# Turning the second product of the first layer: tokens stationary for five of six blocks, and another issue plan

## The chip, the cores and the metric

The kernel runs on one core of a Trainium2 chip. The time is device microseconds of one execution; the kernel before has a median of 624.69 us over three runs (620.73 to 627.0). A profiled execution of it took 617.57 us, of which 615.9 us lie between its first and its last instruction (the span).

## The reference, cut to what matters

Three layers follow one another. A delta-rule attention runs over 768 steps for 2 x 8 heads of width 48 and yields x, 1536 tokens by 384. The first layer is a dense one with a rational activation:

```
h = x @ w_in                        # 1536 x 384 by 384 x 2048
P = a[0] + a[1]*h + a[2]*h*h + a[3]*h*h*h
Q = 1 + |b[0]|*|h| + |b[1]|*h*h
g = P / (Q + 1e-6)
x = g @ w_out                       # the second product: 1536 x 2048 by 2048 x 384
```

The second layer sends each token to one of 8 experts by the argmax of x @ w_gate, and computes gate * (relu(x @ w1[e]) @ w2[e]) for it. Every token's row has to be known before the last expert lists are complete.

## The kernel before, in words

**Attention.** The sequence is cut into 12 chunks of 64 steps. Groups of four chunks share a triangular solve on VectorE (solve, L249, 31 pairs of operations per group, lines L264 and L267). Then every chunk runs a chain of small TensorE products (lower, tk, qk, u, s, y, x), with ScalarE copies between them. x_mm (L387) puts the result of a chunk, split in a high and a low f16 part, into the block's x tiles, with features on the partitions.

**First layer.** Two chunks make a block of 256 tokens; there are six blocks. A block has eight tiles, each of two groups of 128 hidden features (w_in's columns) by 256 tokens. Per tile, s1 runs 18 f16 matmuls of 256 columns (L454); ScalarE, GpSimd and VectorE evaluate the rational function (steps s1, e2, e3), and e3 splits g into gh (ScalarE, L481) and gl = g - gh (GpSimd, L482), both f32r, with hidden features on the partitions and tokens along the free axis. s2 (L485) runs the second product: for each of three groups of 128 output features and each of the two hidden groups, three matmuls (wo_h with gh, wo_h with gl, wo_l with gh), 18 of 256 columns each. The stationary operand is a 128x128 piece of w_out, the moving one is g. Two of the three accumulators share a PSUM bank, which a matmul of zeros over 512 columns (L493) opens. After the eighth tile three ScalarE copies (L505) bring the block's result to x2, features on partitions.

**Weights of the first layer.** w_in and w_out come as float64 and are taken apart by conv (L194) in 16 pieces: four VectorE operations (L189, L190, L191, L199), two ScalarE copies (L198, L201) and one GpSimd subtraction (L202) each. conv_load (L181) brings a piece into a ring of two tiles by a DMA of SyncE's queue, so a later load waits for an earlier piece's conversion. Tile number t of block 0 needs pieces 2t and 2t+1.

**Gate.** gate (L507) is a generator of five steps per block. It multiplies x2 by w_gate (L516, features are the contraction, so x2's layout fits), finds the expert of each token, counts places (place, L567), turns x2 into rows of tokens with six transposes (L547) into PSUM, scales each row by a power of two and writes the rows to DRAM (SyncE DMA). After the last block's gate the expert lists are read back and gathered by row.

**Experts.** 16 DMAs, ScalarE casts (L702) and VectorE subtractions (L703) bring the weights of the first two experts ahead of time, during blocks 4 and 5; their early lists are settled after gate 3 (settle, L615). The others are loaded behind the last list. Each expert has hp products (L746, 256 columns) and y products (L783, 384 columns).

**Order.** All steps up to the last block stand in a dictionary with a time from PLAN, sorted by that time at L949; a step first issues what it needs. The times are only numbers to sort by. The program is then built under a tile framework that arranges the instructions of each engine by a simulated timeline, with the issue order as priority, so that instructions of several steps are mixed on one engine; on the chip every engine works in the order so fixed. In PLAN, `tiles` holds for each block the time of its first tile and the step between tiles, `lags` those of e2, e3 and s2 behind s1, `u` the times of the chunks, `rel` those of a chunk's other steps around it, `solve` the start and the step of each of the three solves, `conv` start and step of pieces 2 to 15, `early` pieces 0 and 1, `lead` how far a load stands ahead of its conversion, `w` the early expert weights, `pre` and `settle` the early experts. behind (L837) also ties a conversion's instructions to the end of an earlier solve: piece 2 to that of solve 0, pieces 3 to 15 to that of solve 1.

Of the kernel before, what the change touches and what calls it, by code (L numbers as in the profile page):

```python
# [7 lines left out]
F32 = mybir.dt.float32  # L8
# [4 lines left out]
AF = mybir.ActivationFunctionType  # L13
# [10 lines left out]
DM = H * D  # L24
# [6 lines left out]
ROW = DM + 1  # L31
BLOCKS = [range(i, i + 2) for i in range(0, 12, 2)]
XS = 0.125
PLAN = {'tiles': ((87.83, 6.95), (160.76, 6.97), (189.73, 5.73), (233.4, 5.29), (280.51, 3.83), (328.46, 2.58)),
 'lags': (8.77, 6.68, 15.19),
 'u': (51.36, 70.55, 88.09, 99.81, 109.31, 135.51, 158.51, 197.55, 219.65, 238.81, 250.88, 281.51),
 'rel': {'kT': 2.63,
         'loads': 4.47,
         'values': -10.66,
         'qk': -3.8,  # L40
         'lower': -5.93,
         'tk': -2.67,
         's': 2.76,
         'y': 2.44,
         'x': 5.8},
 'norm': (-34.08, 36.43, 112.73),
 'solve': ((-7.06, 3.69), (20.76, 8.26), (160.31, 5.92)),
 'gram': ((-1.03, 1.43), (15.51, 2.1), (124.49, 9.18)),
 'qk': (10.43, 33.11),
 'conv': (58.99, 3.27),  # L50
 'early': (8.24, 14.14),
 'lead': 16.47,
 'gate': (1.01, 2.5),
 'w': (354.93, 2.35),
 'experts': 2,
 'behind': 3,
 'masks': 2,
 'copies': 1,
 'settle': 298.54,
 'pre': ((342.38, 356.18, 337.4, 357.65), (326.4, 369.59, 380.06, 389.43)),  # L60
 'hold': 1}
WN = 4
CA = 2
# [12 lines left out]
def attention_moe_moe(ctx, tc, kT, qT, k, v, beta, w_io, a, b, w_gate, w1, w2, out, dbg=None):  # L76
    nc = tc.nc
# [4 lines left out]
    st = ctx.enter_context(tc.tile_pool(name="st", bufs=2))  # L82
# [3 lines left out]
    ps_a = ctx.enter_context(tc.tile_pool(name="ps_a", bufs=2, space=PSUM))  # L86
# [4 lines left out]
    def slot(shape, dt, name):  # L91
        return slots.tile(shape, dt, tag="slot", name=name)
# [7 lines left out]
    wo_h = slot([128, 16, DM], F32R, "wo_h")  # L100
    wo_l = slot([128, 16, DM], F32R, "wo_l")
# [31 lines left out]
    def load_kk(r):  # L133
        kk = st.tile([128, 2, 16, D], F32, tag="raw", name="kk", bufs=2)
        for i in range(2):
            kks[r, i] = kk[:, i]
            nc.sync.dma_start(kks[r, i], k[:, 4 * r + 2 * i:4 * r + 2 * i + 2].rearrange("p c u d -> p (c u) d"))
# [10 lines left out]
    ident = const.tile([128, 128], F32, name="ident")  # L148
# [124 lines left out]
    ends = {}  # L273

    def lower(n, tile_):
# [6 lines left out]
        for p in range(2):  # L282
            lo, hi = slice(64 * p, 64 * p + 32), slice(64 * p + 32, 64 * p + 64)
            for sl, o in ((lo, 0), (hi, 32)):
                if n < PLAN["copies"]:
                    nc.gpsimd.tensor_copy(Z[sl, :, p, o:o + 32], Wu[sl, :, us].rearrange("p t u -> p u t"))
# [46 lines left out]
    def qk(n, tile_):  # L333
# [6 lines left out]
        for p in range(2):  # L340
            o = slice(64 * p, 64 * p + 64)
            if n < PLAN["masks"]:
                nc.vector.tensor_tensor(G[o, :, p, :], g[o], mask[o].unsqueeze(1).to_broadcast([64, NP, C]), ALU.mult)
# [65 lines left out]
    wg = const.tile([128, 3, E], F32, name="wg")  # L409
# [24 lines left out]
    acc, ghl, x2t = {}, {}, {}  # L434
# [50 lines left out]
    def s2(i):  # L485
        blk, js_ = TILES[i]
        w = 512 // len(js_)
        gh, gl = ghl.pop(i)
        if js_[0] == 0:
            pair = ps_a.tile([128, 2, 256], F32, tag="acc", name="acc")  # L490
            acc[blk] = [pair[:, 0], pair[:, 1], ps_a.tile([128, 256], F32, tag="acc", name="acc2")]

            nc.tensor.matmul(pair.rearrange("p a (c b) -> p a c b", c=2), low16[0:1, 0:1].to_broadcast([1, 128]), ones16[0:1].unsqueeze(1).to_broadcast([1, 4, 128]).rearrange("p (a c) b -> p a c b", a=2), start=True, stop=False)  # L493
        for dt in range(3):
            ds_ = slice(128 * dt, 128 * dt + 128)
            for k_, j in enumerate(js_):
                for m, (ww, g) in enumerate(((wo_h, gh), (wo_h, gl), (wo_l, gh))):
                    ends["s2"] = nc.tensor.matmul(  # L498
                        acc[blk][dt][:, 0:w], ww[:, j, ds_], g[:, w * k_:w * k_ + w], start=(dt == 2 and j == 0 and m == 0), stop=(dt > 0 and j == 15 and m == 2)
                    )  # L500
        if js_[-1] == 15:
            x2 = st.tile([128, 3, 256], F32, tag="t64", name="x2", bufs=3)
            x2t[blk] = [x2[:, dt] for dt in range(3)]
            for dt in range(3):
                nc.scalar.activation(x2t[blk][dt], acc[blk][dt], AF.Copy)  # L505

    def gate(blk, tile_, tile_x, tile_p):  # L507

        nt = len(BLOCKS[blk])
        pr = BLOCKS[blk][0] // 2  # L510
        hp = nt // 2
        x2 = x2t.pop(blk)
        lp = tile_([128, nt, E], "lp")
        for i in range(nt):
            for dt in range(3):
                nc.tensor.matmul(lp[:, i, :], x2[dt][:, 128 * i:128 * i + 128], wg[:, dt, :], start=(dt == 0), stop=(dt == 2))  # L516
        lg = sm.tile([128, nt, E], F32, tag="lg", name="lg")
        m = sm.tile([128, nt, 6], F32, tag="m", name="m")

        def bc(i):  # L520
            return m[:, :, i:i + 1].to_broadcast([128, nt, E])

        eib = ei.unsqueeze(1).to_broadcast([128, nt, E])
        w = sm.tile([128, nt, E], F32, tag="w", name="w")
        nc.vector.tensor_reduce(m[:, :, 0:1], lp, AX, ALU.max)
        nc.vector.tensor_tensor(w, lp, bc(0), ALU.is_equal)
        nc.vector.tensor_tensor(w, w, eib, ALU.mult)
        nc.vector.tensor_reduce(m[:, :, 1:2], w, AX, ALU.min)
        oh4 = oh.rearrange("p (b i) e -> p b i e", b=2)[:, :, pr:pr + hp]
        nc.vector.tensor_tensor(  # L530
            oh4, bc(1).rearrange("p (b i) e -> p b i e", b=2), eib.rearrange("p (b i) e -> p b i e", b=2), ALU.is_equal
        )
        nc.vector.tensor_tensor(lg, lp, bc(0), ALU.subtract)
        pl = place(blk, tile_p)
        next(pl)
        nc.scalar.activation(lg, lg, AF.Exp)
        nc.vector.tensor_reduce(m[:, :, 2:3], lg, AX, ALU.add)
        nc.vector.tensor_scalar(m[:, :, 2:3], m[:, :, 2:3], 1e-9, None, ALU.add)
        nc.vector.reciprocal(m[:, :, 2:3], m[:, :, 2:3])
        yield  # L540
        if blk < len(BLOCKS) - 1:
            next(pl)
            yield
        for i in range(nt):
            xp = tile_x([128, DM], "xp2")
            for dt in range(3):
                nc.tensor.transpose(xp[:, 128 * dt:128 * dt + 128], x2[dt][:, 128 * i:128 * i + 128], ident)  # L547
            tt = 6 * (i // hp) + pr + i % hp
            mx = m[:, i, 3:4]
            nc.vector.tensor_reduce(mx, xp, AX, ALU.max, apply_absolute_value=True)  # L550
            nc.vector.tensor_scalar(mx, mx, 2.0 ** -100, None, ALU.max)
            nc.vector.tensor_scalar(mx.bitcast(U32), mx.bitcast(U32), 0x7F800000, None, ALU.bitwise_and)
            nc.vector.reciprocal(m[:, i, 4:5], mx)
            xr = sm.tile([128, ROW], F32, tag="xr", name="xr")
            nc.scalar.activation(xr[:, 0:DM], xp, AF.Copy, scale=m[:, i, 4:5])
            nc.vector.tensor_scalar(xr[:, DM:ROW], m[:, i, 2:3], 1.0 / (MS * MS), mx, ALU.mult, ALU.mult)
            nc.sync.dma_start(rows[128 * tt:128 * tt + 128, :], xr)
            if dbg is not None:
                nc.sync.dma_start(dbg["x2"][128 * tt:128 * tt + 128, :], xr[:, 0:DM])
                nc.sync.dma_start(dbg["sc"][:, tt:tt + 1], mx, allow_slow_non_contiguous=True)  # L560
            yield
        if blk == len(BLOCKS) - 1:
            next(pl)
        yield
# [248 lines left out]
    def add(name, time, needs, f):  # L813
        todo[name] = (time, needs, f)
# [10 lines left out]
    first = {blk: next(i for i in range(len(TILES)) if TILES[i][0] == blk) for blk in range(len(BLOCKS))}  # L825
    tiles_at, lags = PLAN["tiles"], PLAN["lags"]
    T = [tiles_at[blk][0] + (i - first[blk]) * tiles_at[blk][1] for i, (blk, _) in enumerate(TILES)]
    U = PLAN["u"]
    r0 = PLAN["rel"]
    early = NCH and U[1] + r0["x"]  # L830
# [17 lines left out]
    add(("kk", 1), 2.0, [], lambda: load_kk(1))  # L848
    add(("kk", 2), PLAN["norm"][2] - 8, [("norm", 1)], lambda: load_kk(2))
    gens = {r: solve(r) for r in range(3)}  # L850
# [41 lines left out]
    for blk in range(len(BLOCKS)):  # L892
        last = blk == len(BLOCKS) - 1
        i = first[blk] + sum(t[0] == blk for t in TILES) - 1
# [86 lines left out]
    with tc.If(over > SLOTS):  # L981
# [3 lines left out]
        for e in range(E):  # L985
            run(weights(e, got2))
            for t0, nt in ((0, 2), (2, 1)):
                x = expert_x(gather(e, t0, nt, idx3), a_tile)
# [61 lines left out]
```

## Time and profile before

| | us |
|---|---|
| median of three runs | 624.69 (620.73 to 627.0) |
| profiled execution | 617.57 |
| its span | 615.9 |
| TensorE matmul busy (6197 instructions) | 520.5, 85% of the span |
| TensorE weight loads busy | 438.9, 71% |
| VectorE busy (868) | 470.8, 76% |
| ScalarE busy (773) | 396.2, 64% |
| GpSimd busy (282) | 289.2, 47% |
| mean granted TensorE clock | 0.953 of full speed |

The busy time of TensorE is of pipelined matmuls, each recorded from its start to its modelled end; what a matmul costs in a row of them is the distance from start to start. PE is the matmul side of TensorE, PEld its weight loads, DVE VectorE, ACT ScalarE, POOL GpSimd, SP SyncE. The granted clock is 1.00 at 2.4 GHz and 0.50 at 1.2 GHz.

### The profile page before, as it was taken

The page shows a single profiled execution, that of the slowest core. Times are in us where ns is not written, and L with a number is a line of the kernel's source. Part 1 is how long each engine was busy: PE and PEld are TensorE (multiplying, and loading weights), DVE is VectorE, ACT ScalarE, POOL GpSimd, SP SyncE. Part 2 cuts the span into 40 slices and gives each one's busy share as a digit, 9 for nine tenths or more (in the row PEclk, how much of TensorE's full clock was granted, in tenths as well). Part 3 has the DMA queues.
Part 4 walks back from the last instruction along what each step waited for, and adds up shares of the span by engine and source line. Part 5 has one row for each costly group of instructions (what it writes and reads, how often), then busy time and mean ns, then how long its engine had stood idle before and what let it go on. Part 6 is the DMA issues. An engine that isn't in the chain of part 4 may idle for free.

```text
span 615.9 us, 15199 instructions
## 1 busy us (share of the span) xinstructions
PE 520.5 (85%) x6197; PEld 438.9 (71%) x6197; DVE 470.8 (76%) x868; ACT 396.2 (64%) x773; POOL 289.2 (47%) x282
## 2 busy tenths in 40 slices
PE   5514995787998999887999999988897799799993
PEld 5514773576777988776888888878786687577761
DVE  4999999999886799997486367899965588873320
ACT  6844665777799776559868779877662477661110
POOL 8402115966965475455576445747752231212111
PEclk9999997889698899998999999989999699999998
DMA  9901313744621002010000100651002798861000
GB/s 254 262 28 56 88 41 108 199 142 129 190 98 41 1 1 57 12 40 1 14 15 28 28 15 20 201 174 59 27 27 93 223 298 281 280 219 41 16 17 30
DMA packets 42159, 59.33 MB, mean 96 GB/s; under 512 B 25550, under 2 KB 29172, under 8 KB 42082
## 3 DMA queue, kind: packets, MB, share of 16 engines
q1 hardware_dynamic: 40034, 52.78, 28.8%
q0 software_dynamic: 2048, 5.52, 2.7%
q8 instruction: 50, 0.82, 0.5%
q14 instruction: 27, 0.22, 0.1%
HBM read 52.76 MB, written 6.30 MB: 96 GB/s over the span
## 4 chain that ended last, share of the span: by engine, by line
DVE 34%; PE 31%; ACT 12%; DMA 9%; issue 7%; POOL 4%; SPq 0%; POOLq 0%; ACTq 0%; DVEq 0%
PE y L783 7%; DVE A L264 7%; PE acc L498 6%; DVE A L267 6%; PE hp L746 6%; PE h L454 5%; DMA ws<-in_w_dram 5%; DVE h L473 2%; DVE pf L464 2%; ACT A L288 2%; DVE pf L463 2%; DVE ew L703 2%; DVE pf L472 2%; DVE t L190 2%; ACT ew L702 2%
## 5 line engine op out<-in xcount | busy, mean ns | idle before, releaser
L454 PE MATMUL h<-x,wi 128*128 128x256 f16 x864 | 114.2, 280 | 15.8 <-ACT wi L198 7.4
L454 PEld LDWEIGHTS <-wi 128*128 128x128 f16 x864 | 79.8, 100 | 32.3 <-ACT wi L198 8.1
L482 POOL TENSOR_TENSOR gl<-pf,gh 128x512 fp32r<-128x512 f32 x48 | 65.1, 1357 | 63.4 <-ACT gh L481 59.5
L498 PE MATMUL acc<-gl,wo_h 128*128 128x256 f32 x288 | 85.9, 302 | 2.0 <-POOL gl L482 2.0
L498 PE MATMUL acc<-gh,wo_h 128*128 128x256 f32 x288 | 83.7, 306 | 1.7 <-ACT gh L481 1.7
L498 PE MATMUL acc<-gh,wo_l 128*128 128x256 f32 x288 | 83.1, 292 | 0.0
L703 DVE SCALAR_TENSOR_TENSOR ew<-ws,ew 128x768 f16<-128x768 f32 x64 | 62.2, 986 | 12.8 <-ACT ew L702 12.7
L461 POOL TENSOR_SCALAR zf<-za,cf 128x512 f32<-128x512 f32 x48 | 44.3, 924 | 51.1 <-ACT za L459 50.6
L702 ACT ACTIVATE ew<-ws 128x768 f16<-128x768 f32 x64 | 52.5, 841 | 20.7 <-DMA ws<-in_w_dram 20.1
L462 POOL TENSOR_TENSOR zf<-zf,za 128x512 f32<-128x512 f32 x48 | 64.2, 1337 | 3.4
L746 PE MATMUL hp<-dx,ew 128*128 128x256 f16 (+1 forms) x576 | 60.7, 268 | 4.9 <-DVE hl L752 4.4
L746 PEld LDWEIGHTS <-ew 128*128 128x128 f16 x576 | 52.9, 102 | 12.1 <-issue 5.6
L498 PEld LDWEIGHTS acc<-gl,wo_h 128*128 128x128 f32 x288 | 57.7, 200 | 3.7 <-POOL gl L482 2.8
L498 PEld LDWEIGHTS acc<-gh,wo_h 128*128 128x128 f32 x288 | 55.4, 199 | 4.5 <-ACT gh L481 2.6
L498 PEld LDWEIGHTS acc<-gh,wo_l 128*128 128x128 f32 x288 | 57.8, 201 | 0.3
L783 PE MATMUL y<-ew,hh 128*128 128x384 f16 x224 | 56.1, 327 | 0.0
L789 POOL DMA_INDIRECT out_dram<-yo,idx x16 | 18.0, 1124 | 77.0 <-DVE yo L787 62.7
L472 DVE SCALAR_TENSOR_TENSOR pf<-pf,cf,h 128x512 f32<-128x512 f32 x48 | 35.5, 740 | 19.0 <-ACT h L471 18.8
L264 DVE TENSOR_TENSOR A<-A,A 128x31 f32<-128x31 f32 (+15 forms) x93 | 42.9, 461 | 2.5
L463 DVE TENSOR_TENSOR pf<-pf,h 128x512 f32<-128x512 f32 x48 | 32.6, 680 | 13.2 <-ACT pf L460 13.2
L267 DVE TENSOR_TENSOR A<-A,A 128x31 f32<-128x31 f32 (+15 forms) x93 | 40.4, 434 | 2.4
L470 ACT ACTIVATE za<-zf,qc 128x512 f32<-128x512 f32 x48 | 34.5, 719 | 11.4 <-POOL zf L462 11.2
(174 smaller groups left out, 1199.3 us busy)
## 6 DMA issues: line engine op xcount, KB each, us to landing
ws<-in_w_dram SPq DMA_DIRECT2D x64, 384.0 KB, 3.9
raw<-in_w_io_dram SPq DMA_DIRECT2D x16, 768.0 KB, 4.0
rows<-xr SPq DMA_DIRECT2D x12, 192.5 KB, 2.4
kk<-in_k_dram SPq DMA_DIRECT2D x6, 384.0 KB, 4.6
A<-in_k_dram SPq DMA_DIRECT2D x24, 96.0 KB, 3.1
v<-in_v_dram SPq DMA_DIRECT2D x12, 192.0 KB, 3.9
A<-in_qT_dram SPq DMA_DIRECT2D x24, 96.0 KB, 2.7
A<-in_kT_dram SPq DMA_DIRECT2D x10, 192.0 KB, 3.8
```

The lines of the kernel that those rows point to most:

```text
L264: nc.vector.tensor_tensor(tmp, A[:, j, n:32].unsqueeze(2).to_broadcast([128, m, n]), T[:, j:n, 0:n].to_broadcast([128, m, n]), ALU.mult)
L267: nc.vector.tensor_tensor(T[:, n:32, 0:n], T[:, n:32, 0:n], tmp, ALU.add)
L454: s1_last[i] = nc.tensor.matmul(h[:, w * m:w * m + w], ww[:, kt, js], x[:, kt, 0:w], start=(n == 0), stop=(n == 8))
L462: nc.gpsimd.tensor_tensor(zf, zf, za, ALU.mult)
L463: nc.vector.tensor_tensor(pf, pf, h, ALU.mult)
L472: nc.vector.scalar_tensor_tensor(pf, pf, cf[:, 0:1], h, ALU.add, ALU.mult)
L482: nc.gpsimd.tensor_tensor(gl, pf, gh.bitcast(F32), ALU.subtract)
L498: ends["s2"] = nc.tensor.matmul(acc[blk][dt][:, 0:w], ww[:, j, ds_], g[:, w * k_:w * k_ + w], start=(dt == 2 and j == 0 and m == 0), stop= ...
L702: nc.scalar.activation(ws[:, 2 * m, cs], s, AF.Copy, scale=MS)
L703: nc.vector.scalar_tensor_tensor(ws[:, 2 * m + 1, cs], s, MS, ws[:, 2 * m, cs], ALU.mult, ALU.subtract)
L746: nc.tensor.matmul(hp[:, g, 0:ns], w[:, kt, 128 * (f + g):128 * (f + g) + 128], xx[:, kt, 0:ns], start=(n == 0), stop=(n == 8))
L783: nc.tensor.matmul(y, hx[f // 4][:, f % 4, cs], w[:, f, :], start=(n == 0), stop=(n == 23))
```

## The change

For blocks 0 to 4 the second product is turned. The stationary operand is now a piece of gh or gl (128 hidden features by 128 tokens), the moving operand is a whole row block of w_out (128 hidden features by 384 output features). A tile then has 12 matmuls of 384 columns where it had 18 of 256. They run in the order wo_h with gh, wo_l with gh, wo_h with gl. The result has tokens on partitions: two accumulators of 384 columns, each a PSUM tile of its own, no matmul of zeros, and two ScalarE copies to x2 where there were three.

The gate of such a block begins with a new first step: six transposes of x2 and two ScalarE copies of 384 columns into xT, which the product with w_gate then reads. The six transposes that stood later in the gate fall away; the row steps read x2 in SBUF and no longer a PSUM tile. The gate keeps five steps: transposes; gate product and expert; counting; both row groups; the rest. Block 5 is computed and gated as before.

PLAN gets other numbers throughout. Sorted, they put conversions 3 to 13 ahead of the y, s and x steps of chunks 0 and 1 (before, they stood among the chunk steps), the steps of solve 2 3.59 apart instead of 5.92, so that its end stands ahead of s2 of tile 11 and no longer behind that of tile 16, block 0's first tile behind chunk 2's x step, settle behind s2 of tile 37 instead of tile 32, and the early expert weights closer together. A moved conversion takes its DMA load with it.

```diff
--- before.py
+++ after.py
@@ -31,33 +31,35 @@
 ROW = DM + 1
 BLOCKS = [range(i, i + 2) for i in range(0, 12, 2)]
 XS = 0.125
-PLAN = {'tiles': ((87.83, 6.95), (160.76, 6.97), (189.73, 5.73), (233.4, 5.29), (280.51, 3.83), (328.46, 2.58)),
- 'lags': (8.77, 6.68, 15.19),
- 'u': (51.36, 70.55, 88.09, 99.81, 109.31, 135.51, 158.51, 197.55, 219.65, 238.81, 250.88, 281.51),
- 'rel': {'kT': 2.63,
-         'loads': 4.47,
+
+BYTOK = range(5)
+PLAN = {'tiles': ((94.62, 6.95), (151.99, 6.94), (188.36, 5.73), (232.03, 5.29), (276.15, 3.92), (344.39, 2.58)),
+ 'lags': (8.77, 6.68, 15.4),
+ 'u': (50.59, 69.78, 81.54, 98.48, 107.98, 124.54, 157.18, 195.04, 218.05, 237.74, 249.51, 282.48),
+ 'rel': {'kT': 2.41,
+         'loads': 4.55,
          'values': -10.66,
          'qk': -3.8,
          'lower': -5.93,
          'tk': -2.67,
-         's': 2.76,
-         'y': 2.44,
-         'x': 5.8},
- 'norm': (-34.08, 36.43, 112.73),
- 'solve': ((-7.06, 3.69), (20.76, 8.26), (160.31, 5.92)),
- 'gram': ((-1.03, 1.43), (15.51, 2.1), (124.49, 9.18)),
- 'qk': (10.43, 33.11),
- 'conv': (58.99, 3.27),
- 'early': (8.24, 14.14),
+         's': 10.18,
+         'y': 3.45,
+         'x': 7.22},
+ 'norm': (-36.92, 54.42, 110.21),
+ 'solve': ((-5.44, 3.69), (31.55, 6.74), (156.04, 3.59)),
+ 'gram': ((-1.03, 1.72), (14.91, 1.55), (123.21, 9.13)),
+ 'qk': (10.43, 32.45),
+ 'conv': (58.22, 0.02),
+ 'early': (8.43, 7.71),
  'lead': 16.47,
  'gate': (1.01, 2.5),
- 'w': (354.93, 2.35),
+ 'w': (364.51, 1.45),
  'experts': 2,
  'behind': 3,
  'masks': 2,
  'copies': 1,
- 'settle': 298.54,
- 'pre': ((342.38, 356.18, 337.4, 357.65), (326.4, 369.59, 380.06, 389.43)),
+ 'settle': 310.33,
+ 'pre': ((362.66, 372.11, 354.38, 372.47), (338.34, 382.38, 397.83, 407.42)),
  'hold': 1}
 WN = 4
 CA = 2
@@ -486,6 +488,22 @@
         blk, js_ = TILES[i]
         w = 512 // len(js_)
         gh, gl = ghl.pop(i)
+        if blk in BYTOK:
+            if js_[0] == 0:
+                acc[blk] = [ps_a.tile([128, DM], F32, tag="acc", name="acct") for _ in range(2)]
+            for m, (ww, g) in enumerate(((wo_h, gh), (wo_l, gh), (wo_h, gl))):
+                for t in range(2):
+                    for k_, j in enumerate(js_):
+                        o = w * k_ + 128 * t
+                        ends["s2"] = nc.tensor.matmul(
+                            acc[blk][t], g[:, o:o + 128], ww[:, j, :], start=(j == 0 and m == 0), stop=(j == 15 and m == 2)
+                        )
+            if js_[-1] == 15:
+                x2 = st.tile([128, 2, DM], F32, tag="t64", name="x2", bufs=3)
+                x2t[blk] = x2
+                for t in range(2):
+                    nc.scalar.activation(x2[:, t], acc[blk][t], AF.Copy)
+            return
         if js_[0] == 0:
             pair = ps_a.tile([128, 2, 256], F32, tag="acc", name="acc")
             acc[blk] = [pair[:, 0], pair[:, 1], ps_a.tile([128, 256], F32, tag="acc", name="acc2")]
@@ -510,10 +528,26 @@
         pr = BLOCKS[blk][0] // 2
         hp = nt // 2
         x2 = x2t.pop(blk)
+        if blk in BYTOK:
+            xT = st.tile([128, 2, DM], F32, tag="t64", name="xT", bufs=3)
+            for i in range(nt):
+                xp = tile_x([128, DM], "xp2")
+                for dt in range(3):
+                    nc.tensor.transpose(xp[:, 128 * dt:128 * dt + 128], x2[:, i, 128 * dt:128 * dt + 128], ident)
+                nc.scalar.activation(xT[:, i], xp, AF.Copy)
+            yield
+
+            def col(i, dt):
+                return xT[:, i, 128 * dt:128 * dt + 128]
+        else:
+
+            def col(i, dt):
+                return x2[dt][:, 128 * i:128 * i + 128]
+
         lp = tile_([128, nt, E], "lp")
         for i in range(nt):
             for dt in range(3):
-                nc.tensor.matmul(lp[:, i, :], x2[dt][:, 128 * i:128 * i + 128], wg[:, dt, :], start=(dt == 0), stop=(dt == 2))
+                nc.tensor.matmul(lp[:, i, :], col(i, dt), wg[:, dt, :], start=(dt == 0), stop=(dt == 2))
         lg = sm.tile([128, nt, E], F32, tag="lg", name="lg")
         m = sm.tile([128, nt, 6], F32, tag="m", name="m")
 
@@ -542,9 +576,12 @@
             next(pl)
             yield
         for i in range(nt):
-            xp = tile_x([128, DM], "xp2")
-            for dt in range(3):
-                nc.tensor.transpose(xp[:, 128 * dt:128 * dt + 128], x2[dt][:, 128 * i:128 * i + 128], ident)
+            if blk in BYTOK:
+                xp = x2[:, i]
+            else:
+                xp = tile_x([128, DM], "xp2")
+                for dt in range(3):
+                    nc.tensor.transpose(xp[:, 128 * dt:128 * dt + 128], col(i, dt), ident)
             tt = 6 * (i // hp) + pr + i % hp
             mx = m[:, i, 3:4]
             nc.vector.tensor_reduce(mx, xp, AX, ALU.max, apply_absolute_value=True)
@@ -558,7 +595,8 @@
             if dbg is not None:
                 nc.sync.dma_start(dbg["x2"][128 * tt:128 * tt + 128, :], xr[:, 0:DM])
                 nc.sync.dma_start(dbg["sc"][:, tt:tt + 1], mx, allow_slow_non_contiguous=True)
-            yield
+            if blk not in BYTOK or i:
+                yield
         if blk == len(BLOCKS) - 1:
             next(pl)
         yield
```

## Rows read from the trace of the kernel before

**Rows 1.** Busy time by stretch, us; (x) counts; then granted clock, DMA share, GB/s.

```profile
92.00:168.00 76.00, 58.72 (x811) 47.44 (x810) 73.82 (x85) 55.57 (x118) 55.28 (x41) 0.84 0.51 154
168.00:222.00 54.00, 50.97 (x648) 44.71 (x644) 42.75 (x82) 47.97 (x98) 33.45 (x34) 0.94 0.15 42
222.00:282.00 60.00, 53.56 (x704) 46.02 (x702) 59.14 (x107) 37.46 (x77) 31.43 (x30) 1.00 0.11 28
282.00:290.00 8.00, 5.58 (x85) 4.86 (x86) 4.90 (x8) 7.84 (x15) 3.90 (x4) 0.93 0.01 2
290.00:400.00 110.00, 109.52 (x1446) 96.50 (x1446) 72.96 (x146) 88.76 (x176) 65.47 (x67) 0.99 0.15 45
400.00:440.00 40.00, 33.01 (x276) 29.28 (x275) 39.50 (x79) 28.34 (x51) 26.60 (x28) 0.96 0.33 100
440.00:464.00 24.00, 24.00 (x234) 21.87 (x234) 15.81 (x33) 14.78 (x27) 11.50 (x10) 1.00 0.07 25
482.00:541.00 59.00, 53.98 (x483) 44.07 (x483) 49.41 (x76) 40.96 (x64) 15.09 (x13) 0.93 0.85 267
```

**Rows 2.** The chain that ended last, in order of time: start, length, what.

```profile
275.46 1.06 DVE A L264
...
315.87 2.59 PE acc L498 x20
...
473.15 7.79 DMA xd<-rows,idx
...
557.76 7.80 PE y L783 x48
```

**Rows 3.** The second product alone (L498) by stretch: PE busy, PEld busy, counts, clock.

```profile
92.00:168.00 76.00, 15.32 (x90) 13.12 (x90) 0.84 0.51 154
168.00:222.00 54.00, 17.38 (x109) 15.86 (x109) 0.94 0.15 42
282.00:290.00 8.00, 0.70 (x3) 0.70 (x4) 0.93 0.01 2
290.00:400.00 110.00, 43.33 (x295) 37.81 (x295) 0.99 0.15 45
```

**Rows 4.** Timeline of PE: start, us, engine, line, operation, count.

```profile
290.53 0.41 PE L498 MATMUL acc<-gl,wo_h 128*128 128x256 f32 x1
290.75 0.41 PE L498 MATMUL acc<-gh,wo_l 128*128 128x256 f32 x1
...
296.20 0.94 PE L454 MATMUL h<-x,wi 128*128 128x256 f16 x7
297.06 0.32 PE L359 MATMUL U<-A,A 112*64 112x48 f32 x2
...
309.28 1.50 PE L516 MATMUL lp<-wg,x 128*128 128x8 f32 x12
...
311.22 0.28 PE L498 MATMUL acc<-gl,wo_h 128*128 128x256 f32 x1
311.34 0.28 PE L498 MATMUL acc<-gh,wo_l 128*128 128x256 f32 x1
```

**Rows 5.** All engines by stretch, as in Rows 1, around the first timeline rows.

```profile
290.00:292.00 2.00, 2.00 (x11) 2.00 (x11) 2.00 (x4) 1.92 (x5) 1.63 (x3) 0.50 0.00 0
```

**Rows 6.** Groups by line: busy us, mean ns; idle before, releaser.

```profile
L498 PE MATMUL acc<-gl,wo_h 128*128 128x256 f32 x288 | 85.9, 302 | 2.0 <-POOL gl L482 2.0
...
L505 ACT ACTIVATE x<-acc 128x256 f32<-128x256 f32 x18 | 5.9, 381 | 4.4 <-PE acc L498 4.3
L385 ACT ACTIVATE ys<-Y 128x384 f32<-128x384 f32 x12 | 5.8, 480 | 0.4 <-PE Y L383 0.3
```

**Rows 7.** One conversion's four VectorE operations (of the same view).

```profile
L191 DVE SCALAR_TENSOR_TENSOR t<-raw,t 128x768 uint32<-128x768 uint32 x16 | 20.3, 1271 | 0.1
L190 DVE SCALAR_TENSOR_TENSOR t<-raw,t 128x768 uint32<-128x768 uint32 x16 | 18.6, 1169 | 0.1
L199 DVE SCALAR_TENSOR_TENSOR wi<-t,wi 128x384 f16<-128x384 f32 x16 | 15.6, 975 | 0.1
L189 DVE TENSOR_SCALAR t<-raw 128x768 uint32<-128x768 uint32 x16 | 13.4, 845 | 1.3 <-DMA raw<-in_w_io_dram 1.3
```

**Rows 8.** The first product alone (L454) by stretch, as Rows 3.

```profile
92.00:168.00 76.00, 17.63 (x108) 9.53 (x105) 0.84 0.51 154
```

## The prediction

> **What bounds the kernel now.** I begin with the busy times by stretch, because no engine bounds the whole span. From 92 to 168 us DVE works 73.8 of 76 us [rows 1]: there the conversions of the weights stand beside block 0's tiles, and PE has 17 us to spare. From 168 to 222 PE works 51.0 of 54 and DVE only 42.8. From 222 to 282 DVE is full again (59.1 of 60), with solve 2 among the tiles. Then comes the stretch that matters most: from 290 to 400 PE is busy for 109.5 of 110 us, DVE for 73.0 and ACT for 88.8. From 400 to 440 DVE has 39.5 of 40 (expert weights beside tiles), from 440 to 464 PE has all of it, with block 5 alone left [rows 1]. The chain that ended last says the same in order of time: solve operations of DVE up to 275, PE rows such as 20 matmuls of L498 in one piece at 315.9, the gather of the last list at 473.2, expert products at the end [rows 2]. What lies behind the gather (482 to 541 with DMA at 0.85 of its share [rows 1], then products) is not touched; it starts when block 5's gate ends. So the question is how much earlier block 5's gate ends.
>
> **Part 1, the product itself.** Its price is the distance from start to start, not the recorded 0.28 us. At full clock it is 311.34 - 311.22 = 0.120 us for 256 columns [rows 4], so a tile's 18 matmuls take 2.16 us. For 384 columns there is no f32r row. The nearest is the experts' y product, 384 columns of f16 with a weight load for each: 7.80 / 48 = 0.1625 us [rows 2]. That is the lower end: 12 x 0.1625 = 1.95 us. The upper end scales the 0.120 with the columns, 0.180 us, and 12 x 0.180 = 2.16 us, no gain at all. Which end is near depends on what the 0.120 is made of, stream or weight load. Two rows bear on it. At the half clock (granted 0.50 [rows 5]) the distance is 290.75 - 290.53 = 0.22, so the stream of 256 columns sets it there (256 / 1.2 GHz = 0.213); at full clock the stream alone would be half of that, 0.107, and 0.120 is more. And the gate product streams 8 columns only, yet 12 of its f32 matmuls start about (1.50 - 0.28) / 11 = 0.111 us apart [rows 4] (0.28, the length of one recorded matmul, stands for the last one's tail): a load of 128 f32 columns costs about that by itself. So 0.120 is a weight load with little added, and under 384 columns it hides. I take 0.1625: 0.21 us saved per tile, 8.4 us over 40 tiles at full clock. At half clock nothing is saved (18 x 0.213 = 12 x 0.320).
>
> The Trainium skill ("TensorE: Matmul & The Clock Gate", section LDWEIGHTS) gives a load of 128 columns 107 ns, and its section "Back-to-back issue gap" gives 256 columns 109 ns and 384 columns 162.5. By these figures both forms of a tile would take 1.95 to 1.96 us and the part would gain nothing. The trace disagrees for f32r: 0.120, not 0.109 [rows 4]; the measurement decides, and what stands above uses the rows alone.
>
> How much of it is open? Where DVE is full, PE time saved is waiting time. I count the second product in the stretches where DVE is not full: 109 + 3 + 295 matmuls [rows 3], which is 407 / 18 = 22.6 tiles, all of blocks 0 to 4. That is 22.6 x 0.21 = **4.75 us**. The other 17.4 tiles (3.65 us) lie under DVE: 0 to 3.65, and as DVE is busy 97 to 99% there I take 0.
>
> **Part 2, small removals.** The matmul of zeros has 512 columns; at the y rate that is 0.217 us [rows 2], five go, three of them in open stretches: 0.65 us. PE stood 2.0 us in all before products that needed gl [rows 6]; it was the second operand in line and is now needed only for the last third, some 8 x 0.1625 = 1.3 us later. Between 0 and 2.0; I take 0.5, as most of the 2.0 lies where DVE is behind anyway.
>
> **Part 3, the gate.** ACT copied 3 x 0.381 = 1.14 us and will copy 2 x 0.480 for x2 and 2 x 0.480 for xT, 1.92 us [rows 6]: 0.78 us more per block, 3.9 in all. ACT has 21 us to spare from 290 to 400 and 6 from 168 to 222 [rows 1], which cover it; uncovered, in the open blocks, it would be 2.3. The transposes are as many as before and only move. The gate product now waits for a round from PE to ACT and back; what stands behind it on PE waits too. The present gate has the same kind of wait (x2's copy) inside the full PE stretch from 290 to 400 without visible idle time [rows 1], since other steps' matmuls are mixed in, as seven of s1 before two of a chunk [rows 4]. So 0; uncovered, two copies and a backlog of one more, 1.5 us a gate, 7.5 in all. SyncE's row DMAs stay in the last gate steps; block 5's gate, the only one on the chain, is unchanged.
>
> **Part 4, the plan.** Solve 2 gets ahead of more tiles. PE idles 2.4 us from 282 to 290 [rows 1], behind the solve's end [rows 2]; an earlier end could remove that, or, by pushing tile work back on DVE, add as much. Between -2.4 and 2.4 I take a gain of 1.2. The conversions ahead of chunk steps are costed at nothing: DVE must do all 16 before block 0 ends in either order and is full there. What that costs if it is not so is a rival. Settle and the early weights move inside blocks 4 and 5; DVE's work there is the same and I take 0.
>
> **Sum.** 4.75 + 0.65 + 0.5 + 1.2 = 7.1 us off the profiled execution's 617.57. That execution is 7.1 us below the median of the runs, so against 624.69 the forecast is **617.6 us**.
>
> **The rivals.** *The product does not get shorter*: f32r streams at 0.180 per 384 columns. Then part 1 is 0 and 2.35 us remain: 622.3. For it: 0.120 exceeds the 0.111 of the bare load; against it: the half clock row. (The Trainium skill's figures, quoted above, end at this same time by the other road, a cheaper product before.) *The saving turns into waits*: in the open stretches PE then stands behind DVE or ACT, part 1 and the solve's move come to nothing, and ACT's extra copies in the open blocks are uncovered: 624.69 - 0.65 - 0.5 + 2.3 = 625.8. For it: ACT has 48.0 of 54 us from 168 to 222 and DVE is full on both sides; against it: from 290 to 400, where 16.4 of the 22.6 tiles lie, DVE has 37 us free [rows 1]. *More is opened*: all 8.4 us, zeros 1.1, gl 2.0 and the solve's 2.4 count, 13.9: 610.8. *The conversions starve PE*, on the slow side: 11 conversions (pieces 3 to 13) cost 1.27 + 1.17 + 0.98 + 0.85 = 4.26 us of DVE each [rows 7], 46.9 us together. If DVE really does them ahead of the x steps of chunks 0 and 1, the first tile starts that much later, and the chunks' input DMAs stand behind loads on SyncE's queue that wait for the ring, GpSimd's subtractions ahead of its chunk work. From 92 to 168 PE now does 108 matmuls of s1 and 90 of s2 [rows 8, 3], 108 x 0.108 (256 of y's 384 columns) + 90 x 0.120 = 22.5 us. Between 46.9 / 76 of it, 13.9 us, and all of it would go behind 168, where PE is nearly full; the middle, 18.2, less 7.1 gives 635.8. It makes the kernel slower by 1% from 13.3 us pushed back. Against it: engines mix steps by readiness [rows 4], and each conversion waits for its load.
>
> **How the numbers follow.** The forecast has 0.46 (its own range 613 to 621, four fifths of it over 1% faster), no shorter product 0.10, turned into waits 0.18, more opened 0.10, starved 0.16. A measurement of this kernel can tell about 1% from no change, here 6.2 us, below 618.4 or above 630.9. Faster: 0.37 + 0.10 = 0.47. Same: 0.09 + 0.10 + 0.18, less 0.01 for a gate that costs its 7.5, 0.36. Slower: 0.16 + 0.01 = 0.17. The range is 607 to 633: it takes in the opened case's 610.8 with its spread and the near end of the starved one, and leaves out some 0.15.
>
> **What would show it.** Starts 0.16 us apart for the turned products at full clock (0.18 says the first rival); PE still full from about 290 to 400 but with block 5's last s2 before 459, not 464; no PE idle time ahead of xT's copies; s1's first tile among the conversions, before 100 us. Wrong would be: first tile past 110, or PE idle in the middle stretch, behind DVE or ACT.

## The result, and the profile after

The changed kernel takes 614.16 us in the median of five runs (610.97 to 617.21), the kernel before 624.69 beside it: a ratio of 0.986 with an interval of 0.982 to 0.990. That is 10.5 us less, where 7.1 were forecast. Timed twice more beside other kernels it had 0.979 (0.974 to 0.984) and 0.985 (0.979 to 0.990).

The profiled execution took 612.29 us, its span is 610.6 us, 5.3 less than before. The profiled execution of before was one of the fastest of its kind (617.57 against a median of 624.69), so the pair of traces shows only half of the median's gain; it tells where, by stretches. Two later traces of the same changed kernel (the runs after_again and after_yard of the experiments) took 615.85 and 616.57 us and show how far one execution may be trusted. First the busy times by stretch of the kernel after, in the columns of [rows 1]:

```profile
92.00:168.00 76.00, 61.00 (x871) 47.07 (x868) 73.92 (x89) 60.06 (x126) 56.89 (x42) 0.89 0.48 149
168.00:222.00 54.00, 48.59 (x637) 40.96 (x636) 44.89 (x83) 49.24 (x103) 35.24 (x33) 0.97 0.20 56
222.00:282.00 60.00, 56.10 (x555) 47.94 (x554) 59.48 (x119) 38.13 (x73) 36.91 (x36) 0.97 0.09 22
282.00:290.00 8.00, 4.38 (x91) 3.80 (x91) 4.90 (x8) 7.86 (x14) 1.28 (x3) 0.88 0.01 2
290.00:400.00 110.00, 106.93 (x1354) 92.00 (x1349) 76.16 (x151) 94.21 (x185) 64.19 (x67) 0.97 0.18 52
400.00:440.00 40.00, 38.05 (x324) 34.93 (x323) 36.60 (x80) 27.18 (x48) 27.66 (x28) 0.95 0.29 91
440.00:464.00 24.00, 23.15 (x242) 20.44 (x240) 12.18 (x36) 11.51 (x21) 7.49 (x9) 1.00 0.07 25
```

Against [rows 1], PE is no longer quite full from 290 to 400 (106.9 for 109.5; 107.5 and 107.9 in the two later traces). From 400 to 440 it is fuller here (38.1 for 33.0), but in the later traces only a little (34.2 and 34.4). Block 5's last second product starts at 455.7 us:

```profile
L516 PE MATMUL acc<-gh,wo_l x48: 278/283/283, 419.7 to 455.7; 128*128 128x256 f32 x48
```

In the later traces it starts at 459.4 and 460.7. Before, PE had second products of block 5 up to the end of the stretch that closes at 464:

```profile
463.50 0.28 PE L498 MATMUL acc<-gh,wo_l 128*128 128x256 f32 x1
```

The gather of the last list, at 473.15 in [rows 2], is at 465.68 in the chain of waits after, and the last expert products are the chain's end as before:

```profile
398.69 6.84 PE acct L498 x24
...
465.68 7.17 DMA xd<-rows,idx
```

So 7.5 us are gained up to the gather, and 2.2 of them are lost again behind it in this execution, among the experts' weights and products that the change does not touch. In the two later traces the gather starts at 471.0 and 471.1, some 2 us before that of the kernel before, whose trace is one of its fastest executions. What is gained is gained ahead of the gather; by how much, the medians say better than any pair of traces.

The turned product in the timeline of PE (start, us, line, count), in a stretch where matmuls follow without a hole:

```profile
340.23 0.85 PE L498 MATMUL acct<-wo_l,gh 128*128 128x384 f32 x4
340.93 0.85 PE L498 MATMUL acct<-wo_h,gl 128*128 128x384 f32 x4
341.62 0.85 PE L498 MATMUL acct<-wo_h,gh 128*128 128x384 f32 x4
```

Eight starts from 340.23 to 341.62: 0.174 us each. The prediction took 0.1625 and named 0.180 as the end at which the product saves nothing. A tile's 12 matmuls take 2.09 us where 18 took 2.16 [rows 4]: 0.07 us less, 2.9 us over 40 tiles at full clock and not 8.4.

The gate's copies and the product's waits, by line (busy, mean ns, idle before):

```profile
L498 PE MATMUL acct<-wo_h,gl 128*128 128x384 f32 x160 | 39.1, 356 | 2.1 <-POOL gl L484 2.1
...
L536 PE MATMUL xp<-ident,x 128*128 128x128 f32 x30 | 5.0, 287 | 0.5 <-ACT x L505 0.5
...
L505 ACT ACTIVATE x<-acct 128x384 f32<-128x384 f32 x10 | 4.7, 492 | 0.1
...
L537 ACT ACTIVATE xT<-xp 128x384 f32<-128x384 f32 x10 | 4.6, 489 | 0.1
```

PE stood 0.5 us in all before the new transposes, and ACT's copies take 0.49 us each, as reckoned. But PE still stands 2.1 us before products that need gl (2.6 in both later traces), as much as in [rows 6]: seen as waits, the later need of gl brought nothing.

### The profile page after: what moved, and what is told of

Its sections match the earlier page's. It is cut to its first block, busy times and chain, and to the rows that moved or that the text cites. A ratio compares the mean times of both kernels' runs of the same rounds, so it can differ in the third digit from the quotient of the medians.

```text
span 610.6 us, 14736 instructions
## 1 busy us (share of the span) xinstructions
PE 511.2 (84%) x5952; PEld 425.5 (70%) x5952; DVE 464.3 (76%) x868; ACT 401.0 (66%) x778; POOL 289.7 (47%) x282
## 4 chain that ended last, share of the span: by engine, by line
PE 37%; DVE 31%; DMA 12%; ACT 10%; issue 5%; POOL 2%; SPq 0%; POOLq 0%; DVEq 0%; ACTq 0%
PE h L456 8%; PE acct L498 7%; DMA ws<-in_w_dram 6%; PE y L821 6%; DVE A L266 6%; DVE A L269 5%; PE hp L784 4%; DMA raw<-in_w_io_dram 3%; ACT A L290 2%; DVE h L475 2%; DVE pf L465 2%; DVE ew L741 2%; PE acc L516 2%; DVE pf L474 2%; DVE pf L466 2%
## 5 line engine op out<-in xcount | busy, mean ns | idle before, releaser
L456 PE MATMUL h<-x,wi 128*128 128x256 f16 x864 | 117.1, 284 | 16.5 <-DVE wi L201 5.5
L463 POOL TENSOR_SCALAR zf<-za,cf 128x512 f32<-128x512 f32 x48 | 42.1, 876 | 52.6 <-ACT za L461 52.2
L498 PE MATMUL acct<-wo_h,gh 128*128 128x384 f32 x160 | 42.2, 379 | 1.7 <-ACT gh L483 1.6
L498 PE MATMUL acct<-wo_h,gl 128*128 128x384 f32 x160 | 39.1, 356 | 2.1 <-POOL gl L484 2.1
L323 POOL TENSOR_TENSOR A<-v,nrm 64x384 f32<-64x384 f32 x24 | 23.2, 967 | 35.8 <-PE S L373 26.3
L290 ACT ACTIVATE A<-A 32x256 f32<-32x256 f32 x44 | 28.7, 651 | 16.3 <-DVE A L272 13.1
L789 ACT ACTIVATE hh<-hp 128x512 f16<-128x512 f32 (+1 forms) x32 | 16.9, 536 | 32.9 <-PE hp L784 32.9
L462 ACT ACTIVATE pf<-h,cf 128x512 f32<-128x512 f32 x48 | 37.2, 775 | 1.0 <-POOL gl L484 0.9
```

The source lines that it names most:

```text
L456: s1_last[i] = nc.tensor.matmul(h[:, w * m:w * m + w], ww[:, kt, js], x[:, kt, 0:w], start=(n == 0), stop=(n == 8))
L498: ends["s2"] = nc.tensor.matmul(acc[blk][t], g[:, o:o + 128], ww[:, j, :], start=(j == 0 and m == 0), stop=(j == 15 and m == 2))
```

## The experiments

**The two halves.** Three kernels on one chip: the changed one, the plan without the turn, the turn without the plan.

```diff
 plan_alone
-BYTOK = range(5)
+BYTOK = range(0)
 turn_alone
 PLAN = {  # every entry as in the kernel before
```

> The changed kernel itself, timed beside the two halves of the change: about 0.986 of the kernel before by every theory (614 us). It is the yardstick for the other runs of this call.

> The new issue plan with the second product as before (no block turned). Theory A (the turned product saves little PE time: starts 0.1735 us apart in the changed kernel's trace, so 18 x 0.120 - 12 x 0.1735 = 0.08 us per tile, 3.1 us in all; the plan does the rest): 6 to 7 us below the kernel before, ratio 0.989 to 0.991. Theory B (the turn with its later need of gl does it all): ratio 1.000. Theory C (each half is of use only with the other, as the plan is fitted to the turned program): slower than before, ratio above 1.003.

> Five blocks turned, with the plan of before. Theory A: 3.1 us for the product and 1 us for the matmuls of zeros at most, so 0 to 4 us below the kernel before, ratio 0.993 to 1.000. Theory B: 10 us below, ratio 0.984. Theory C: slower than before, ratio above 1.003.

| | median us | ratio to before | interval |
|---|---|---|---|
| before | 627.88 | | |
| plan alone | 633.09 | 1.010 | 1.006 to 1.013 |
| turn alone | 622.09 | 0.993 | 0.989 to 0.996 |
| both | 614.79 | 0.979 | 0.974 to 0.984 |

The ratios are not the quotients of these medians and differ a little from them. The halves do not add up. The turn alone is worth 627.88 x 0.0075 = 4.7 us (2.4 to 7.1 by its interval), which agrees with 2.9 for the product and 1.1 for five matmuls of zeros. The plan alone costs 6 us, and on the turned program it brings 622.09 - 614.79 = 7.3. Theory C held for the plan but not for the turn. Theory A's bound for the turn was a little low (4.7 against 0 to 4), and for the plan alone it fell: it had 6 to 7 us below the kernel before, where 6 above were measured. Theory B fell for both.

**What the distance of 0.120 us consists of.** The same sums in matmuls of 128 columns (cut; the matmuls of zeros that open the accumulators are left out here):

```diff
-acc[blk][t], g[:, o:o + 128], ww[:, j, :], ...
+for d in range(0, DM, 128):
+    acc[blk][t][:, d:d + 128], g[:, o:o + 128], ww[:, j, d:d + 128], ...
```

> The turned product with each 384-column stream cut in three of 128 columns (each opened by a matmul of zeros), so the same sums in 36 matmuls and 36 weight loads a tile. It measures what the 0.120 us of 256 columns consists of. If an f32r matmul costs its stream and a fixed 13 ns (0.107 + 0.013 = 0.120, 0.160 + 0.013 = 0.173), starts are 0.066 us apart at full clock. If the load of 128 f32 columns sets a floor, as the prediction took it, they are 0.111 to 0.120 us apart. The kernel as a whole gets slower by some 10 us in the first case and some 60 us and more in the second.

It took 707.0 us in its one run, 79 more than before. In its timeline:

```profile
300.72 1.54 PE L501 MATMUL acct<-wo_h,gh 128*128 128x128 f32 x12
302.10 1.50 PE L501 MATMUL acct<-wo_l,gh 128*128 128x128 f32 x12
303.44 1.50 PE L501 MATMUL acct<-wo_h,gl 128*128 128x128 f32 x12
```

From 302.10 to 303.44 twelve starts, 0.112 us each: there is a floor, and it is the 0.111 that the gate product's rows gave. Not every matmul of 128 columns with a load of its own has it. In the trace of the kernel before, early expert products in f16 have 144 matmuls and 144 loads of 128 columns, and start (469.60 - 466.58) / 54 = 0.056 us apart:

```profile
466.58 3.18 PE L766 MATMUL ehp<-ax,ew 128*128 128x128 f16 x54
469.60 0.17 PE L580 MATMUL pp<-oh,low 128*128 128x16 f16 x1
```

So the floor belongs to the f32 operands. That it is their load is argued and not tested apart: 128 streamed columns need only half of it, and a recorded load of 128 columns is 0.192 us long for the f32r products and 0.098 for the f16 ones. But 0.112 lies below 0.120. The stream explains the two longer sizes: 256 columns take 0.120 and 384 columns 0.174, so 0.054 for 128 more columns, which is 128 / 2.4 GHz (0.053), and some 0.013 us per matmul are left on top at either size. The f16 products have 0.1625 for 384 columns [rows 2], 0.0025 on top. By these distances the second product before the change was bound by its stream and this fixed part, with the load 0.008 us behind it. What the turn saves is six fixed parts a tile, 6 x 0.013 = 0.08 us.

**Parts of the plan put back.**

```diff
 late_old:  tiles[4], tiles[5], u[11], w, settle, pre              as before
 mid_old:   tiles[1..3], u[6..10], norm[2], solve[2], gram[2]      as before
 early_old: tiles[0], u[0..5], conv, early, norm[0..1],
            solve[0..1], gram[0..1], qk                            as before
 (rel and lags stay as changed in all three)
 all_turned:
-BYTOK = range(5)
+BYTOK = range(6)
```

> The changed kernel with the plan's late entries as before: first tiles of blocks 4 and 5, chunk 11, early expert weights, settle, early experts. The plan brings 7 us on the turned program (622.1 to 614.8). Theory D (the gain is in the end of the first layer: block 5 begins when chunk 11's x is there, 405 us in the changed kernel, 411 in the one with the turn alone): this run gives most of it back, 5 to 8 us above the changed kernel, some 621. Theory F (the whole plan is fitted to the program, so that any part of it put back costs): 3 to 15 us above, as much as the other two. Theory M (the gain is in the middle): within 2 us of the changed kernel.

> The changed kernel with the plan's middle as before: first tiles of blocks 1 to 3, chunks 6 to 10, norm, grams and steps of solve 2. Theory D: within 2 us of the changed kernel. Theory M (solve 2 ahead of more tiles and tiles 16 to 20 some 10 us earlier is what pays): 5 to 8 us above it. Theory F: 3 to 15 us above.

> The changed kernel with the plan's early entries as before: first tile of block 0, chunks 0 to 5, conversions, norms, grams and steps of the first two solves. The prediction costed the conversions' new places at nothing, and the first tile is at 92 us in both kernels: theories D and M say within 2 us of the changed kernel. Theory F: 3 to 15 us above.

> All six blocks turned, plan as changed. Eight more tiles at 12 x 0.1735 = 2.08 for 18 x 0.120 = 2.16 us: 0.6 us less, a matmul of zeros 0.2 less; but block 5's gate is on the chain and gets a round to ScalarE more (six transposes 0.65 us, copies of some 1 us) before its product with w_gate. If that round is exposed: 1 to 2 us above the changed kernel. If the row steps, which no longer need their transposes, give it back: within 1 us. If all entries of a plan are fitted (theory F): any sign, up to 10 us.

| | median us | ratio to before (623.65) | interval |
|---|---|---|---|
| late entries back | 620.02 | 0.995 | 0.991 to 0.998 |
| middle entries back | 624.25 | 1.001 | 0.997 to 1.004 |
| early entries back | 622.46 | 1.002 | 0.998 to 1.006 |
| all six blocks turned | 612.19 | 0.982 | 0.977 to 0.986 |

Each third put back costs 8 to 12 us against the fourth kernel of the table, and 6 to 10 against the 614.2 us of the changed one, which was not timed beside these. The whole plan brings 7.3, so the three losses add up to some three times the gain. Neither theory D nor M holds: there is no one place in which the plan gains. Theory F, a plan that is of use as a whole, stands.

**A small disturbance, and the order of the operands.**

```diff
 jitter: tiles, u, norm, early, solve, gram, w, settle, pre: each start
         time moved by a random amount, up to 0.5 us
 gl_second:
-for m, (ww, g) in enumerate(((wo_h, gh), (wo_l, gh), (wo_h, gl))):
+for m, (ww, g) in enumerate(((wo_h, gh), (wo_h, gl), (wo_l, gh))):
```

> The changed kernel again, as the yardstick of this call: 0.979 to 0.986 of the kernel before, as twice already.

> The changed kernel with every start time of the plan moved by up to 0.5 us either way, drawn at random; by the sorted lists this exchanges 49 pairs of steps, where the plan of before and the new one differ in 948 (late entries put back 116, middle 252, early 609). Theory F1 (the arrangement of instructions is so sensitive that any change of order costs what the fitted plan brings): 4 to 10 us above the changed kernel. Theory F2 (it needs a real change of the stages' places to lose the gain): within 2.5 us of the changed kernel.

> The changed kernel with the turned product's three thirds in the order of before: wo_h with gh, wo_h with gl, wo_l with gh. gl is then needed 4 matmuls, some 0.7 us, earlier. The prediction gave the later need 0.5 us, bounds 0 to 2. If so: 0 to 2 us above the changed kernel; a larger difference of either sign says that the altered arrangement of the rest, not the wait for gl, makes it.

> All six blocks turned, now beside the changed kernel on the same chip. The first time it had 0.982 of the kernel before, the changed kernel 0.979 and 0.986 in its two timings: within 2 us of the changed kernel, if that was right.

| | median us | ratio to before (623.52) | interval |
|---|---|---|---|
| the changed kernel | 614.17 | 0.985 | 0.979 to 0.990 |
| jitter | 613.07 | 0.984 | 0.978 to 0.990 |
| gl second | 627.2 | 1.007 | 1.004 to 1.010 |
| all six blocks turned | 612.20 | 0.982 | 0.977 to 0.987 |

The jitter, of which one draw was timed, costs nothing (theory F2): the arrangement is not so touchy that any exchange of neighbours loses the gain. The order of three operands is worth 13 us, six times the upper end of what was expected. And it is not PE standing before gl. In the run with gl second, PE's rows are:

```profile
L498 PE MATMUL acct<-wo_h,gl 128*128 128x384 f32 x160 | 39.1, 362 | 0.9 <-POOL gl L484 0.9
```

0.9 us, less than the 2.1 of the changed kernel. Nor is it the granted clock: executions with gl second at 0.930 to 0.938 took 624.9 to 631.0 us, those of the changed kernel at 0.897 to 0.903 took 614.4 to 618.2. What differs is the arrangement on the engines. Two stretches with gl second:

```profile
400.00:440.00 40.00, 32.74 (x243) 28.31 (x242) 34.98 (x69) 25.79 (x45) 25.45 (x22) 0.91 0.19 51
440.00:464.00 24.00, 21.07 (x211) 18.73 (x209) 16.09 (x32) 14.89 (x25) 14.86 (x16) 1.00 0.11 34
```

PE is busy for 53.8 us from 400 to 464, where the three traces of the changed kernel have 57.4 to 61.2. Over all seven stretches from 92 to 464 it is 333.6 us with gl second, 332.3 with the turn alone and 334.5 to 338.2 in the changed kernel (sums of such lines), too little difference for 13 us. The end of solve 2 moved as well. The row of its closing transpose (count, shortest/median/longest, first and last start), first with gl second, then in the changed kernel:

```profile
L272 DVE STREAM_TRANSPOSE A<-A x3: 1245/1245/1246, 49.5 to 270.8; 128x1024 f32<-128x1024 f32 x3
```

```profile
L272 DVE STREAM_TRANSPOSE A<-A x3: 1246/1246/1246, 49.4 to 280.0; 128x1024 f32<-128x1024 f32 x3
```

With gl second DVE finishes the solve 9 us earlier (12 to 13 against the later traces) and the tiles behind it fall back: tile 19's rational function starts at 271.2 us, in the changed kernel at 245.9 to 249.2. But that is not yet the loss. The start of a tile's rational function (its first ScalarE operation) and of the last gather, in us, from the traces:

| | changed, three traces | jitter | gl second | early entries back | middle entries back |
|---|---|---|---|---|---|
| tile 19 | 245.9 to 249.2 | 259.3 | 271.2 | 272.3 | 260.2 |
| tile 24, first of block 3 | 288.0 to 291.3 | 289.6 | 303.1 | 303.4 | 290.4 |
| tile 32, first of block 4 | 355.1 to 358.0 | 354.6 | 357.6 | 357.1 | 362.6 |
| tile 40, first of block 5 | 407.7 to 410.2 | 410.2 | 416.6 | 409.0 | 418.8 |
| last gather | 465.7 to 471.1 | 468.8 | 479.4 | 479.7 | 479.5 |

By tile 32 the kernel with gl second has caught up. What it loses, it loses between there and the gather. The early entries put back lose all of it behind tile 40, the middle ones begin to lose before tile 32, and the jitter is 10 us late at tile 19 without any loss. In the changed kernel 15 of the 40 turned products start before their gl is done, with gl second 7, as counted in the two traces; with the jitter it is 12, so this count does not measure the loss either. The runs show that a matmul's place in a group changes when PE, DVE and ScalarE come to their steps, since nothing else was edited. By which decision of the simulated timeline it does so was not followed, and whether the old plan with the turned product, or with the old product, would also lose or gain by the place of gl was not tried. The 13 us are shown under the new plan, their path is not. If the plan is fitted to the program with gl last, they are theory F once more.

All six blocks turned is level with the changed kernel: 612.2 for 614.2, with intervals that overlap nearly whole. Its ratio was 0.982 both times, between the 0.979 and the 0.986 of the changed kernel.

## Why the prediction was right, and where it was not

**The direction and the time** were right: 614.2 measured for 617.6, inside the range, and on the side that had the largest chance. That is luck in part. Parts 1 to 3 forecast 5.9 us for the turn, and the turn alone brought 4.7 (2.4 to 7.1); but part 1 was too large, and part 4, forecast at 1.2 for the plan, was worth 7.3 by a way that the prediction did not have.

**Part 1 was mis-sized.** The step that failed is "So 0.120 is a weight load with little added, and under 384 columns it hides". Of the two rows it rested on, the gate product's was read rightly: the load costs 0.112. The half-clock row was not: load and stream are equally long there (last section), so it could not tell them apart. The prediction noted that 0.120 exceeds *both*, 0.107 and 0.111, the second as a point for its first rival, but it gave the rest no price. The rest over the stream is a part of 0.013 us that stays under 384 columns. Reading the 0.120 as stream plus fixed part would have given 0.160 + 0.013 = 0.173. The saving was 2.9 us, not 8.4; by the prediction's own share of 22.6 open tiles in 40 that is 1.6, not 4.75. The first rival, "the product does not get shorter", was nearer to the truth than the forecast's own first term. The Trainium skill ("TensorE: Matmul & The Clock Gate", sections LDWEIGHTS and "Back-to-back issue gap") gives a load its columns divided by 1.2 in ns, which is an estimate of 107 ns for 128, and adds 2.5 ns to the stream in what it calls the isolated gap. The f16 rows agree with the 2.5 ns (0.1625 us for 384 columns); the f32r rows have 13 ns there, and 112 for the load, while f16 matmuls of 128 columns with a load each start 56 ns apart, which 107 would not allow if each load had to be waited for. The gain of nothing that follows from these figures came closer to the measured saving than the rows' reading did, but by a cheaper product before, where the rows show a dearer one after.

**Part 2.** The matmuls of zeros could not be told apart from the rest of the turn. "it was the second operand in line and is now needed only for the last third" was priced at 0.5 us as a wait of PE, bounds 0 to 2.0. As a wait it brought nothing (2.1 after, 2.0 before). Undone under the new plan, it costs 13 us, with another order on the engines. The bounds had looked only at idle rows of the engine that waits, and no such row shows these 13.

**Part 3 held.** PE waited 0.5 us for the copies of x2 and not for those of xT, and the gates cost nothing that can be seen.

**Part 4 failed in its mechanism.** The forecast's 1.2 us came from an earlier end of solve 2, but the solve's closing transpose starts at 280.0 us after (282.8 and 283.3 in the later traces), and before it started at 277.3:

```profile
L270 DVE STREAM_TRANSPOSE A<-A x3: 1245/1246/1247, 49.1 to 277.3; 128x1024 f32<-128x1024 f32 x3
```

Nor did PE's idle time from 282 to 290 go away: it was 2.4 us and is 3.6. The plan is worth 7 us on the turned program, minus 6 on the old one, and is of use only as a whole. A rival that the prediction did not have, "the plan fits only the changed program", would have said so.

**The rivals.** The conversions do not starve PE: the first tile's first product starts at 89.6 us in the kernel after, 88.7 before, and the early entries put back make it slower, not faster. The rows, first before and then after:

```profile
L454 PE MATMUL h<-x,wi x864: 269/273/437, 88.7 to 448.9; 128*128 128x256 f16 x173
```

```profile
L456 PE MATMUL h<-x,wi x864: 269/273/437, 89.6 to 441.9; 128*128 128x256 f16 x173
```

"The saving turns into waits" was half true of part 1: PE lost 2.6 us of its full stretch from 290 to 400. Of what was to be seen, the first tile before 100 us came true, and no idle time of PE ahead of xT's copies; the last second product before 459 came true in the first trace (455.7) and not in the two later ones (459.4, 460.7); starts 0.16 us apart did not.

## What to carry to other kernels

When a measured distance lies above every bound you can name, the remainder is a cost of its own; find a second size for it before you scale. A change that comes with an order written for it cannot be priced as the sum of both: time each half alone, and the halves will show if one is a loss without the other. Where a planner arranges the engines, the place of a late operand in its group can be worth far more, under the plan that came with it, than the waits for it that the trace shows. And a second trace of the same kernel tells which differences between two traces mean anything.

## What the runs showed of the hardware that was not expected

At full clock an f32r matmul costs its columns at 2.4 GHz and about 13 ns more (0.120 us for 256, 0.174 for 384), an f16 one about 2.5 ns more (0.1625 for 384, 0.056 for 128). With 128 f32r columns, and a load of 128 for each, matmuls start no closer than 0.112 us at full clock, and this floor slows down with the clock. In the kernel with 128-column products, a stretch with a granted clock of 0.50 has these rows:

```profile
208.14 0.47 PE L501 MATMUL acct<-wo_h,gl 128*128 128x128 f32 x1
...
210.41 1.54 PE L501 MATMUL acct<-wo_h,gl 128*128 128x128 f32 x6
```

(1.54 - 0.47) / 5 = 0.214 us from start to start, where the stream of 128 columns would need 0.107 at 1.2 GHz: at half clock the load is as long as 256 streamed columns (0.213). So the half-clock row of the prediction did not show the stream alone, as it was read; load and stream are equally long there.
